# A 2496-point transform split 39 x 64 by index maps: one constant second-stage factor, and dispatch weights moved through it without transposes

## The chip, the cores and the metric

The kernel runs on one core of a Trainium2 chip. The metric is the device time of one execution in microseconds (us). Engines are named as in the profile: PE (TensorE matmuls; PEld are its weight loads), DVE (VectorE), ACT (ScalarE), POOL (GpSimd), and SP (SyncE), whose queue issues every DMA of this kernel. All arithmetic is float32 or its single-pass form fp32r.

## What is computed

A circular convolution along the sequence (by a real FFT, a filter and the inverse), and on its output a soft mixture of experts with 8 experts of 4 slots:

```
X = np.fft.rfft(x, axis=1)                 # x: 8 x 2496 x 256
y = np.fft.irfft(X * (filt_r + 1j * filt_i)[None], n=2496, axis=1)
x = y.reshape(19968, 256)
logits = x @ phi                           # 19968 x 32
d = exp(logits - logits.max(0));  d /= d.sum(0) + 1e-09
slot_input = d.T @ x                       # 32 x 256, "dispatch"
slot_out[e] = max(slot_input[e] @ w1[e], 0) @ w2[e]
c = exp(logits - logits.max(1));  c /= c.sum(1) + 1e-09
out = c @ slot_out                         # "combine"
```

## The kernel before

The tokens of a batch never leave the spectrum: the filtered spectrum is kept (tiles `y`), the logits of the spectrum are transformed back to tokens, and the dispatch weights of the tokens are transformed to the spectrum, where they are contracted with `y`.

**The transform.** Token n is written 64*s1 + s2. Stage one is a 39-point transform over s1, of which 20 values t = 0..19 are kept (the others are conjugates). Stage two is, for each t, a product with a 128x128 factor `b_t[:, t]` (64 values of s2, real and imaginary, against 64 bins, real and imaginary). The twiddle between the stages depends on t, so the 20 factors differ. At the start `build_b` (L641) makes 19 of them from two constant matrices and a cosine and a sine per row, one ACT multiply (L647, tile `bt`) and one DVE multiply-add (L648) each; the constants arrive in `be_t` and `b_t[:, 0]` by `load_b` (L688). Their transposes, which the inverse needs, are made later by `build_minv` (L650): four PE transposes, an ACT copy and a small POOL copy for each of 5 quarters.

**Startup.** Batch 0 goes through `first_unit` (L285): 11 units of 4 matmuls (L291) with a PSUM tile from `ps_s1` (2 buffers), each copied to `spec` by ACT (even units, L298) or DVE (odd, L296). A unit of `build_b` is written behind each of the first ten. Then `turn_ash` (L300) transposes `spec`, which needs all 11 units. Ahead of it, three matmuls (L705) on a tile of zeros run on PE while nothing has been loaded.

**The main loop** (L763) has 80 slots, 10 for each batch. A slot runs `x_unit` (L358): 4 matmuls (L365), two DVE multiplies with the filter tables `fr_t` and `fi_t` (L378, L379), a DVE or POOL add (L381), a POOL subtraction (L382), and for the first slot of a batch the Nyquist bin (L384); two slots later `t_unit` (L386) transposes the result into `y` (L392, L394) and makes logits of it (L403). Beside it go stage-one units of later batches: ACT and POOL split x into a high and a low part (`xh` L323, `xl` L324), three matmuls (L334), a copy (L335), a DMA to DRAM, and a DMA back in the order that stage two needs (`ash`, L355). The tables come by `load_tables` (L663), two values of t at a time.

**The chains.** For each group of batches, (0,1), (2,3), (4,5), (6), (7), `chain` (L416) is cut into pieces by `yield`, two of which are run after each slot. It turns logits to tokens (`v1` L449 with `minv_t`, `v` L469, `lg` L476), takes maxima, makes the weights `d` (L514, L515), turns them to the spectrum (`u` L532, `u2` L549, `dt` L563, `dd` L579), sums them (`z` L587), contracts them with `y` (`s` L607) and makes the row softmax (L628 to L636). `dt` has for each batch and t a matmul that loads 32 columns of `u2` as weights and streams `b_t[:, t]`; its result lies the wrong way round, so `dd` transposes it.

**The tail.** The expert weights (`w`, 64 DMAs of 256 KB, L746 and L748) are put into buffers that `y`, `ash` and the filter tables leave, so they wait for the last `x_unit` and the `s` of the last groups. Then the experts run (L833 to L863) and the combine writes the output, 20.4 MB.

What stands where on each engine is decided by a scheduler that simulates the program; each engine, SP too, then works its list in order.

Of the kernel before, what the change touches and what calls it, by code (L numbers as in the profile page):

```python
# [54 lines left out]
WM = 3  # L55
MV = 6
# [17 lines left out]
def freq_of(t, h, m):  # L74

    if t == 0:
        return N1 * m if h == 0 else None
    return N1 * m + (t if h == 0 else N1 - t)


def shape_constants():
# [10 lines left out]
    bm = np.zeros((N2, 2, NT, 2, 2, 32))  # L92
    for t in range(NT):
        for h in range(2):
            for m in range(32):
                f = freq_of(t, h, m)
                if f is None:
                    continue
                ph = 2 * np.pi * ((f * s2) % SEQ) / SEQ
                co, si = np.cos(ph), np.sin(ph)  # L100
                bm[:, 0, t, 0, h, m] = co
                bm[:, 0, t, 1, h, m] = -si
                if t:
                    sg = 1.0 if h == 0 else -1.0
                    bm[:, 1, t, 0, h, m] = sg * si
                    bm[:, 1, t, 1, h, m] = sg * co
    ph = np.pi * (s2 % 2)
    bm[:, 0, 0, 1, 0, 0] = np.cos(ph)
    bm = bm.reshape(P, NT, P)
    be = np.zeros((2, N2, 2, 2, 2, 32))  # L110
    for h in range(2):
        sg = 1.0 if h == 0 else -1.0
        for m in range(32):
            ph = 2 * np.pi * (((m + h) * s2) % N2) / N2
            co, si = np.cos(ph), np.sin(ph)
            be[0, :, 0, 0, h, m] = co
            be[0, :, 0, 1, h, m] = -si
            be[0, :, 1, 0, h, m] = sg * si
            be[0, :, 1, 1, h, m] = sg * co
            be[1, :, 0, 0, h, m] = -sg * si  # L120
            be[1, :, 0, 1, h, m] = -sg * co
            be[1, :, 1, 0, h, m] = co
            be[1, :, 1, 1, h, m] = -si
    tw = 2 * np.pi * np.repeat(s2, 2)[:, None] * np.arange(NT)[None] / SEQ
    bt = np.concatenate([bm[:, 0], be[0].reshape(P, P), be[1].reshape(P, P), np.cos(tw), np.sin(tw)], axis=1)
    for t in range(1, NT):
        full = be[0].reshape(P, P) * np.cos(tw[:, t : t + 1]) + be[1].reshape(P, P) * np.sin(tw[:, t : t + 1])
        assert np.abs(full - bm[:, t]).max() < 1e-12
    bh = bm[:, 0, :].copy()
    bh[:, 0] *= 0.5  # L130
    bh[:, 64] *= 0.5
# [16 lines left out]
    wt0 = np.full((P, 1), SCALE)  # L148
    wt0[0] = wt0[64] = SCALE / 2
    put("wt0", wt0)  # L150
    put("bh", bh)
# [27 lines left out]
    return cst.astype(f), off, w1q.astype(f), bt.astype(f)  # L179


CST, OFF, W1Q, BMAT = shape_constants()
KP = N2 + 2


def filter_layout(filt, special_zero):

    idx = np.array([[[freq_of(t, h, m) or 0 for m in range(32)] for h in range(2)] for t in range(NT)])
    a = filt[idx.reshape(NT, 64)]
    a = np.ascontiguousarray(a.reshape(NT, 64, 2, P).transpose(3, 0, 2, 1))  # L190
    if special_zero:
        a[:, 0, :, 0] = 0
    return a.reshape(P, NT * 2 * 64)
# [27 lines left out]
def fft_soft_moe(ctx, tc, x, fr, fi, fny, phi, w1, w2, cst, w1q, bmat, out):  # L221
# [136 lines left out]
    def x_unit(b, c):  # L358
# [4 lines left out]
        for k in range(2):  # L363
            for dh in range(2):
# [3 lines left out]
                    b_t[:, t0 + k, :],  # L368
# [14 lines left out]
        if c == 0:  # L383
            dve.tensor_tensor(out=yt[:, 0:2, 1, 0], in0=ps[:, 0:2, 1, 0], in1=fny_t, op=ALU.mult)  # L384
# [31 lines left out]
    def chain(g):  # L416
# [25 lines left out]
        for t0 in range(0, NT, 7):  # L442
            n = min(7, NT - t0)
            pv = psum([P, 7, KP // 2, 2], f"v1_{g}_{t0}")
            for t in range(t0, t0 + n):
                for b2 in range(nb):
                    for h in range(2):
# [4 lines left out]
                            minv_t[:, t, h * KP : (h + 1) * KP],  # L452
# [100 lines left out]
        NR = NT // 4  # L553
        dt = wk.tile([P, nb * NR, P], F32, tag="ca", name=f"dt_{g}", bufs=1)
        for r0 in range(0, nb * NR, 4):
            n = min(4, nb * NR - r0)
            pd = psum([P, 4, P], f"dt_{g}_{r0}")
            for r in range(r0, r0 + n):
                b2, tr = divmod(r, NR)
                for j in range(4):  # L560
                    t = 4 * tr + j
                    th, ti = divmod(t, HT)
                    pe.matmul(  # L563
                        pd[32 * j : 32 * j + 32, r - r0, :],
                        u2[:, ti, b2, th, :],
                        C("bh") if t == 0 else b_t[:, t, :],
                        start=True,
                        stop=True,
                    )
            act.copy(dt[:, r0 : r0 + n], pd[:, 0:n])  # L570
# [4 lines left out]
        for r0 in range(0, nb * NR, 4):
            n = min(4, nb * NR - r0)
            pd = psum([P, 4, P], f"dd_{g}_{r0}")
            for r in range(n):
                pe.transpose(pd[:, r, :], dt[:, r0 + r, :], ident)  # L579
            dve.tensor_copy(ddf[:, r0 * P : (r0 + n) * P], pd.rearrange("k r q -> k (r q)")[:, 0 : n * P])  # L580
# [4 lines left out]
        for b2 in range(nb):
            for j in range(4):
                pe.matmul(  # L587
                    pz[32 * j : 32 * j + 32, :], dd[:, b2, 0, :], C("e0"), start=(b2 == 0), stop=(b2 == nb - 1)
                )
# [14 lines left out]
        for b2, b in enumerate(bs):  # L604
            for t in range(NT):
# [35 lines left out]
    def build_b(c):  # L641

        for t in range(max(2 * c, 1), 2 * c + 2):
            sin_t = be_t[:, 2 * P + NT + t : 2 * P + NT + t + 1]
            cos_t = be_t[:, 2 * P + t : 2 * P + t + 1]
            tmp = x0p.tile([P, P], F32, tag="bt", name=f"bt_{t}", bufs=3)
            act.mul(tmp, be_t[:, P : 2 * P], sin_t)  # L647
            dve.scalar_tensor_tensor(out=b_t[:, t], in0=be_t[:, 0:P], scalar=cos_t, in1=tmp, op0=ALU.mult, op1=ALU.add)  # L648

    def build_minv(i):  # L650

        pm = ps_c.tile([P, 4, P], F32, tag="c", name=f"minv_{i}")
        for k in range(4):
            pe.transpose(pm[:, k], b_t[:, 4 * i + k, :], ident)
        ts = slice(4 * i, 4 * i + 4)
        act.mul(minv_t[:, ts, 0:P], pm, SCALE)
        if i == 0:
            act.mul(minv_t[:, 0, 0:P], pm[:, 0], C("wt0"))
        pad = minv_t[:, ts, P:].rearrange("c t (k r) -> c t k r", r=2)
        last_k = minv_t[:, ts, P - 2 : P].rearrange("c t (o r) -> c t o r", o=1).broadcast_to([P, 4, KP - N2, 2])  # L660
        pool_e.tensor_copy(pad, last_k)
# [26 lines left out]
    def load_b():  # L688
        sp.dma_start(b_t[:, 0], bmat[:, 0:P])
        sp.dma_start(be_t, bmat[:, P:])  # L690

    be_t = x0p.tile([P, 2 * P + 2 * NT], F32, name="be_t", bufs=1)
# [296 lines left out]
```

## Time and profile before

| what | before |
|---|---|
| median of 3 runs (lowest, highest) | 410.76 us (410.0, 410.95) |
| the profiled execution | 411.57 us |
| its span, first to last instruction | 409.8 us |
| PE, PEld busy | 372.0, 295.6 us |
| DVE, ACT, POOL busy | 279.0, 222.5, 201.1 us |
| moved by DMA | 103.81 MB |
| mean granted PE clock | 0.974 |

The profile has a page, which groups instructions by line, and views that answer a question: the timeline (start, duration, engine, line, operation), the chain of waits (the work that ended last, followed back; each piece with its start and duration), groups of instructions (count, busy time, mean duration, idle time ahead of them), and busy times in chosen stretches. A float32 matmul leaves two records on PE, a transpose or an fp32r matmul one.

### The profile page before, as it was taken

How to read it: one execution, taken by the hardware profiler on the slowest of the kernel's cores; microseconds unless marked ns; L12 is line 12 of the kernel's file. 1: busy time of each engine (PE TensorE's matmuls, PEld its weight loads, DVE VectorE, ACT ScalarE, POOL GpSimd, SP SyncE). 2: the span in 40 equal slices, each digit the busy share in tenths (PEclk: the TensorE clock that was granted, in tenths of full speed). 3: DMA queues.
4: the chain of work that ended last, by engine and by line, in shares of the span. 5: the costliest groups of instructions: out<-in, count | busy, mean ns of one | idle time of the engine just before them, and what ended most of it. 6: DMA issues, size and time to landing. Idle time of an engine off the chain costs nothing.

```text
span 409.8 us, 12706 instructions
## 1 busy us (share of the span) xinstructions
PE 372.0 (91%) x5155; PEld 295.6 (72%) x5155; DVE 279.0 (68%) x500; ACT 222.5 (54%) x479; POOL 201.1 (49%) x234
## 2 busy tenths in 40 slices
PE   6899999989998999999998999989998799988940
PEld 3788888868686867886877688779677534677830
DVE  4566788776999925778997567895549422587740
ACT  5777877766667475855781233461256210466630
POOL 0368979985775586865952155572120300443000
PEclk9999999999999999999999999998998999999985
DMA  7999899998689787987768033333089799199996
GB/s 250 357 279 309 266 332 310 309 369 275 178 258 314 234 254 223 299 300 226 239 194 297 5 106 108 106 98 106 2 298 375 242 281 323 78 416 412 415 416 275
DMA packets 57917, 103.81 MB, mean 253 GB/s; under 512 B 5551, under 2 KB 34607, under 8 KB 55683
## 3 DMA queue, kind: packets, MB, share of 16 engines
q1 hardware_dynamic: 57859, 103.00, 75.4%
q8 instruction: 41, 0.67, 0.7%
q14 instruction: 17, 0.14, 0.1%
HBM read 62.87 MB, written 40.12 MB: 251 GB/s over the span
## 4 chain that ended last, share of the span: by engine, by line
PE 65%; DVE 13%; DMA 10%; ACT 5%; issue 2%; SPq 0%; DVEq 0%; ACTq 0%
PE x L365 16%; PE s L334 11%; PE t L392 7%; DMA w<-in_w 6%; PE out L922 5%; PE s L607 4%; PE l L403 4%; DMA out<-ob 3%; PE dt L563 3%; PE v L449 2%; DVE t L379 2%; DVE yt L378 2%; PE u L532 2%; DVE d L514 2%; PE lg L476 2%
## 5 line engine op out<-in xcount | busy, mean ns | idle before, releaser
L324 POOL TENSOR_TENSOR xl<-xt,xh 117x512 fp32r<-117x512 f32 x77 | 103.6, 1353 | 36.6 <-ACT xh L323 34.0
L365 PE MATMUL x<-b_t,ash 128*128 128x128 f32 x640 | 91.3, 284 | 3.0 <-DVE t L379 2.0
L365 PEld LDWEIGHTS x<-b_t,ash 128*128 128x128 f32 x640 | 81.2, 194 | 12.0 <-issue 5.2
L382 POOL TENSOR_TENSOR yt<-yt,t 128x256 f32<-128x256 f32 x80 | 64.9, 812 | 47.7 <-DVE t L379 30.7
L378 DVE TENSOR_TENSOR yt<-x,fr_t 128x512 f32<-128x512 f32 x80 | 54.8, 685 | 30.4 <-PE x L365 21.1
L394 ACT COPY y<-t 128x512 f32<-128x512 f32 x80 | 46.4, 592 | 37.1 <-PE t L392 31.3
L323 ACT CAST xh<-xt 117x512 fp32r<-117x512 f32 x77 | 47.8, 622 | 29.5 <-PE s L334 19.8
L379 DVE TENSOR_TENSOR t<-x,fi_t 128x512 f32<-128x512 f32 x80 | 54.2, 678 | 0.0
L381 DVE TENSOR_TENSOR yt<-yt,t 128x256 f32<-128x256 f32 x60 | 49.7, 836 | 0.6
L392 PE MATMUL t<-cst_t,yt 128*128 128x128 f32 x320 | 48.5, 276 | 0.0
L335 ACT COPY at<-s 120x512 f32<-120x512 f32 x77 | 45.0, 588 | 1.1 <-PE s L334 1.0
L392 PEld LDWEIGHTS t<-cst_t,yt 128*128 128x128 f32 x320 | 37.1, 141 | 6.5 <-issue 2.7
L334 PE MATMUL s<-xh,w1h 117*120 117x512 f32 x77 | 35.3, 459 | 1.9 <-ACT at L335 1.8
L922 PE MATMUL out<-so_h,st 32*128 32x256 f32 x312 | 30.2, 299 | 3.8 <-ACT st L876 3.2
L381 POOL TENSOR_TENSOR yt<-yt,t 128x256 f32<-128x256 f32 x20 | 16.2, 811 | 32.3 <-DVE t L379 26.0
L334 PE MATMUL s<-xl,w1h 117*120 117x512 f32 x77 | 30.8, 400 | 0.1
L334 PE MATMUL s<-xh,w1l 117*120 117x512 f32 x77 | 30.5, 396 | 0.0
L931 DVE COPY ob<-out 128x512 f32<-128x512 f32 (+1 forms) x40 | 25.2, 672 | 6.3 <-PE out L922 4.9
L922 PEld LDWEIGHTS out<-so_h,st 32*128 32x128 f32 x312 | 23.9, 183 | 6.7 <-ACT st L876 3.5
L922 PE MATMUL out<-so_l,st 32*128 32x256 f32 x312 | 28.0, 277 | 0.0
L931 ACT COPY ob<-out 128x512 f32<-128x512 f32 (+1 forms) x40 | 21.3, 580 | 11.4 <-PE out L922 8.5
L403 PE MATMUL l<-yt,phi_t 128*32 128x128 f32 x640 | 27.1, 278 | 0.4 <-ACT y L394 0.2
(121 smaller groups left out, 576.6 us busy)
## 6 DMA issues: line engine op xcount, KB each, us to landing
xt<-in_x SPq DMA_DIRECT2D x35, 512.0 KB, 5.7
ash<-a_dram SPq DMA_DIRECT2D x70, 256.0 KB, 4.1
out<-ob SPq DMA_DIRECT2D x17, 1024.0 KB, 9.1
a_dram<-at SPq DMA_DIRECT2D x70, 240.0 KB, 5.0
w<-in_w SPq DMA_DIRECT2D x64, 256.0 KB, 5.5
xt<-in_x SPq DMA_DIRECT2D x18, 256.0 KB, 3.1
out<-ob SPq DMA_DIRECT2D x5, 512.0 KB, 12.8
c_dram<-lg SPq DMA_DIRECT2D x2, 643.5 KB
```

Of the source, the lines that this page charges most:

```text
L323: act.copy(xh, xs)
L324: pool_e.tensor_tensor(out=xl, in0=xs, in1=xh.bitcast(F32), op=ALU.subtract)
L334: pe.matmul(ps, w, xx, start=(n == 0), stop=(n == 2))
L365: pe.matmul(ps[:, 2 * k + dh].rearrange("q r c -> q (r c)"), ash[:, k, dh * P : (dh + 1) * P], b_t[:, t0 + k, :], start=True, stop=True,)
L378: dve.tensor_tensor(out=yt, in0=ps, in1=frv, op=ALU.mult)
L379: dve.tensor_tensor(out=t2, in0=ps[:, :, ::-1, :], in1=fiv, op=ALU.mult)
L381: add.tensor_tensor(out=yt[:, :, 1, :], in0=yt[:, :, 1, :], in1=t2[:, :, 1, :], op=ALU.add)
L382: pool_e.tensor_tensor(out=yt[:, :, 0, :], in0=yt[:, :, 0, :], in1=t2[:, :, 0, :], op=ALU.subtract)
L392: pe.transpose(pt[:, k, dh, :], yt[:, c % 2, 2 * k + dh].rearrange("q r c -> q (r c)"), ident)
L394: act.copy(y, pt.rearrange("k p h d -> k p (h d)"))
L922: nc.tensor.matmul(prs[k][:, mm, :], st[q, n // 2, c0 : c0 + P], (so_h, so_l)[n % 2][q, :], start=(n == 0), stop=(n == 3),)
L931: copy(ob[:, nm * k : nm * (k + 1), :], prs[k])
```

## The change

Tokens and bins are mapped so that the twiddle is 1: token (64*s1 + 39*s2) mod 2496, bin t + 39*m with m = (c - t/39) mod 64. The host arranges x and gathers the output by these maps. Then:

- one constant 128x128 factor `b` serves all t; `b_t`, `be_t`, their DMAs, `build_b` and `build_minv` go. The inverse reads the constants `minv` and (for t = 0) `minv0`. The first constant load has 256 columns in place of 129.
- the 64 bins of a t include bins above 1248; there the table holds the mirrored bin, and the imaginary part changes its sign: `load_tables` now has a POOL multiply by -1 on pieces of `fi_t`, 29 in all, 64 of 128 columns for each t of 1 to 19. The Nyquist multiply (L384) goes.
- the dispatch weights go through `b` as one wide matmul per up to 512 columns, with `b` as weights and `u2` streamed; the result is `dd` the right way round, so `dt` and the transposes go. ACT copies it; a DVE multiply halves two rows of t = 0.
- `first_unit` takes its PSUM tiles in turn from two pools (4 buffers in place of 2), and one warm-up matmul runs in place of three.

```
-WM = 3
-MV = 6
+WM = 1
+def token_of(s1, s2):
+    return (N2 * s1 + N1 * s2) % SEQ
+def bin_of(t, c):
+    m = (c - t * pow(N1, -1, N2)) % N2
+    return t + N1 * m
...
+    f = np.array([[bin_of(t, c) for c in range(N2)] for t in range(NT)])
+    a = filt[np.where(f > SEQ // 2, SEQ - f, f)]
+    a[0, N2 // 2 + 1 :] = 0
...
-        ps = ps_s1.tile([P, 2, 2, QP], F32, tag="s1", name=f"s0_{u}")
+        pool, tag = ((ps_s1, "s1"), (ps_x, "x"))[u % 2]
+        ps = pool.tile([P, 2, 2, QP], F32, tag=tag, name=f"s0_{u}")
...
-                    b_t[:, t0 + k, :],
+                    C("b"),
...
-        if c == 0:
-            dve.tensor_tensor(out=yt[:, 0:2, 1, 0], in0=ps[:, 0:2, 1, 0], in1=fny_t, op=ALU.mult)
...
-                            minv_t[:, t, h * KP : (h + 1) * KP],
+                            C("minv" if t else "minv0", h * KP, (h + 1) * KP),
...
-        dt = wk.tile([P, nb * NR, P], F32, tag="ca", name=f"dt_{g}", bufs=1)
...
-                    pe.matmul(
-                        pd[32 * j : 32 * j + 32, r - r0, :],
-                        u2[:, ti, b2, th, :],
-                        C("bh") if t == 0 else b_t[:, t, :],
...
-            act.copy(dt[:, r0 : r0 + n], pd[:, 0:n])
...
-                pe.transpose(pd[:, r, :], dt[:, r0 + r, :], ident)
-            dve.tensor_copy(ddf[:, r0 * P : (r0 + n) * P], pd.rearrange("k r q -> k (r q)")[:, 0 : n * P])
...
+        dd = wk.tile([P, HT, nb, 2, SLOTS], F32, tag="cb", name=f"dd_{g}", bufs=1)
+        for t0 in range(0, HT, SA):
...
+            pe.matmul(
+                pd[:, 0:n],
+                C("b"),
+                u2[:, t0 : t0 + n].rearrange("k t b h e -> k t (b h e)"),
...
+            act.copy(dd[:, t0 : t0 + n].rearrange("k t b h e -> k t (b h e)"), pd[:, 0:n])
+            if t0 == 0:
+                dve.tensor_scalar(
+                    out=dd[:, 0, :, 0, :], in0=dd[:, 0, :, 0, :], scalar1=C("wh"), scalar2=None, op0=ALU.mult
+                )
...
-    def build_b(c):
...
-    def build_minv(i):
...
+        for t in range(lo, hi):
+            for c0, c1 in flip_runs(t) if t else ():
+                sl = fi_t[:, t, :, c0:c1]
+                pool_e.tensor_scalar(out=sl, in0=sl, scalar1=-1.0, scalar2=None, op0=ALU.mult)
...
-        if c == 1:
-            load_b()
...
-            sp.dma_start(cst_t[:, 0 : P + 1], cst[:, 0 : P + 1])
+            sp.dma_start(cst_t[:, 0 : 2 * P], cst[:, 0 : 2 * P])
...
-        if u < CPB:
-            build_b(u)
...
-            if 0 <= n - MV < NT // 4:
-                build_minv(n - MV)
```

`flip_runs(t)` gives the one or two stretches of columns of t whose bin lies above 1248.

Three places show how the lists of the engines change. A row is: line, operation, tile written, tiles read, shape, and a count. Line numbers of the changed kernel are its own; numbers in the names count tiles.

**ACT, from the start**, before. `bt` is half of a factor, `spec` the copy of a unit of batch 0, `xh` the high part of x of batch 1:

```order
L647 ACTIVATE bt_251<-be_t 128x128
L298 COPY spec<-s_0_164 128x2x12x20
L647 ACTIVATE bt_254<-be_t 128x128
L647 ACTIVATE bt_263<-be_t 128x128
L647 ACTIVATE bt_266<-be_t 128x128
L647 ACTIVATE bt_275<-be_t 128x128
L298 COPY spec<-s_2_185 128x2x12x20
L647 ACTIVATE bt_278<-be_t 128x128
L298 COPY spec<-s_4_209 128x2x12x20
L323 CAST xh_0_322<-xt_0_152 117x512
```

and in the changed kernel:

```order
L280 ACT_TABLE_LOAD
L280 COPY spec<-s_0_167 128x2x12x20
L280 COPY spec<-s_2_179 128x2x12x20
L280 COPY spec<-s_4_191 128x2x12x20
L280 COPY spec<-s_6_203 128x2x12x20
L305 CAST xh_0_268<-xt_0_146 117x512
L305 CAST xh_1_272<-xt_0_146 117x512
L280 COPY spec<-s_8_215 128x2x12x20
L280 COPY spec<-s_10_227 128x2x8x20
```

Fourteen `bt` stood ahead of the first copy of `spec`; none is left, and the copies stand first.

**POOL, from the start**, before (`xl` is the low part of x of batch 1, `yt` the filtered spectrum of batch 0):

```order
L324 TENSOR_TENSOR xl_0_323<-xt_0_152,xh_0_322 117x512
L324 TENSOR_TENSOR xl_1_327<-xt_0_152,xh_1_326 117x512
L324 TENSOR_TENSOR xl_2_333<-xt_1_156,xh_2_332 117x512
L324 TENSOR_TENSOR xl_3_346<-xt_1_156,xh_3_345 117x512
L324 TENSOR_TENSOR xl_4_352<-xt_2_160,xh_4_351 117x512
```

and in the changed kernel, where `fi_t` is the imaginary filter table:

```order
L616 TENSOR_SCALAR fi_t<-fi_t 128x2x23
L616 TENSOR_SCALAR fi_t<-fi_t 128x2x9
L306 TENSOR_TENSOR xl_0_269<-xt_0_146,xh_0_268 117x512
L616 TENSOR_SCALAR fi_t<-fi_t 128x2x32
L616 TENSOR_SCALAR fi_t<-fi_t 128x2x5
L616 TENSOR_SCALAR fi_t<-fi_t 128x2x27
L306 TENSOR_TENSOR xl_1_273<-xt_0_146,xh_1_272 117x512
L616 TENSOR_SCALAR fi_t<-fi_t 128x2x28
L616 TENSOR_SCALAR fi_t<-fi_t 128x2x4
L616 TENSOR_SCALAR fi_t<-fi_t 128x2x32
L306 TENSOR_TENSOR xl_2_279<-xt_1_153,xh_2_278 117x512
L306 TENSOR_TENSOR xl_3_295<-xt_1_153,xh_3_294 117x512
```

The sign changes, each behind the load of its table, are mixed in among the first ten low parts.

**PE, dispatch of the third group** (batches 4 and 5), before. The tiles named `u_2` here are `u2` of the program, `cst_t` holds constants (identity, halved factor):

```order
L549 MATMUL u_2_8_4076<-cst_t,u_3906 128x128 x2
L563 MATMUL dt_0_4081<-cst_t,u_2_4032 32x128
L563 MATMUL dt_0_4081<-b_t,u_2_4032 32x128 x15
L563 MATMUL dt_4_4099<-b_t,u_2_4032 32x128 x4
L563 MATMUL dt_4_4099<-cst_t,u_2_4032 32x128
L563 MATMUL dt_4_4099<-b_t,u_2_4032 32x128 x11
L563 MATMUL dt_8_4117<-b_t,u_2_4032 32x128 x8
L579 MATMUL dd_0_4150<-cst_t,dt_4080 128x128 x4
L579 MATMUL dd_4_4156<-cst_t,dt_4080 128x128 x4
L579 MATMUL dd_8_4162<-cst_t,dt_4080 128x128 x2
L587 MATMUL z_4166<-cst_t,dd_4149 32x1 x8
```

and in the changed kernel:

```order
L529 MATMUL u_2_8_3890<-cst_t,u_3720 128x128 x2
L537 MATMUL dd_0_3895<-u_2_3846,cst_t 128x512
L537 MATMUL dd_4_3899<-u_2_3846,cst_t 128x512
L537 MATMUL dd_8_3902<-u_2_3846,cst_t 128x256
L555 MATMUL z_3927<-cst_t,dd_3894 32x1 x8
```

Forty small matmuls and ten transposes become three wide matmuls, at the same place between `u2` and `z`.

More of the change, by code (lines that the diff above doesn't have):

```diff
@@ L43 @@
 NM = BATCH * SQ // P
+KP = N2 + 2
 XC = 4
@@ L90, in shape_constants @@
             w1[:, 1, t] = -np.sin(th)
[L92 to L131, printed above, removed]
+    th = 2 * np.pi * (np.outer(s2, N1 * np.arange(N2)) % N2) / N2
+    co, si = np.cos(th), np.sin(th)
+    bm = np.zeros((N2, 2, 2, N2))
+    bm[:, 0, 0], bm[:, 0, 1], bm[:, 1, 0], bm[:, 1, 1] = co, -si, si, co
+    bm = np.where(np.abs(bm) < 1e-12, 0.0, bm).reshape(P, P)
+    wh = np.ones((P, 1))
+    wh[0] = wh[N2 // 2] = 0.5
+    minv = np.zeros((P, KP * 2))
+    minv[:, 0:P] = SCALE * bm.T
+    minv[:, P:] = np.tile(minv[:, P - 2 : P], (1, KP - N2))
     blocks = []
@@ L147, in shape_constants @@
     put("id", np.eye(P))
[L148 to L151, printed above, removed]
+    put("b", bm)
+    put("wh", wh)
+    put("minv", minv)
+    put("minv0", wh * minv)
     put("w1d", w1d.reshape(KR, 2 * PK * NT))
@@ L178, in shape_constants, with filter_layout, flip_runs @@
     f = np.float32
[L179 to L193, printed above, removed]
+    return cst.astype(f), off, w1q.astype(f)
+CST, OFF, W1Q = shape_constants()
+def filter_layout(filt):
+    f = np.array([[bin_of(t, c) for c in range(N2)] for t in range(NT)])
+    a = filt[np.where(f > SEQ // 2, SEQ - f, f)]
+    a[0, N2 // 2 + 1 :] = 0
+    return np.ascontiguousarray(a.reshape(NT, N2, 2, P).transpose(3, 0, 2, 1)).reshape(P, NT * 2 * N2)
+def flip_runs(t):
+    out = []
+    for c in range(N2):
+        if bin_of(t, c) > SEQ // 2:
+            if out and out[-1][1] == c:
+                out[-1] = (out[-1][0], c + 1)
+            else:
+                out.append((c, c + 1))
+    return out
 def x_layout(x):
-    s2 = np.array([[run_of(i, j) for i in range(NI)] for j in range(PK)])
-    a = x.reshape(BATCH, N1, N2, DIM)[:, :, s2]
+    s1 = np.arange(N1)
     full = np.zeros((BATCH, P, NI, DIM), x.dtype)
-    full[:, 0:KR] = a.transpose(0, 2, 1, 3, 4).reshape(BATCH, KR, NI, DIM)
+    for j in range(PK):
+        for i in range(NI):
+            full[:, j * N1 : j * N1 + N1, i] = x.reshape(BATCH, SEQ, DIM)[:, token_of(s1, run_of(i, j))]
     return full
@@ L587, in chain @@
                 pe.matmul(
[L588 removed]
+                    pz[32 * j : 32 * j + 32, :], dd[:, 0, b2, 0, :], C("e0"), start=(b2 == 0), stop=(b2 == nb - 1)
                 )
@@ L639, in chain @@
             sp.dma_start(c_dram[g], lg_t)
-    def build_b(c):
[L643 to L648, printed above, removed]
-    def build_minv(i):
[L652 to L661, printed above, removed]
     def load_tables(c):
@@ L686, in split_next @@
                 next_x()
[L688 to L692, printed above, removed]
     spec = x0p.tile([P, 2, NT, P], F32, name="spec", bufs=1)
@@ L769, in fft_soft_moe @@
             if n == CPB:
-                sp.dma_start(cst_t[:, P + 1 :], cst[:, P + 1 :])
+                sp.dma_start(cst_t[:, 2 * P :], cst[:, 2 * P :])
             if n == ASH:
```

47 lines of the change are left out of this document (11 added, 36 removed).

## The prediction

> **What bounds the kernel now.** I read the page first, then busy times by stretch, then the chain of waits inside each stretch, and rows of groups where a price was needed. The page gives PE the largest share:
>
> ```profile
> PE 372.0 (91%) x5155; PEld 295.6 (72%) x5155; DVE 279.0 (68%) x500; ACT 222.5 (54%) x479; POOL 201.1 (49%) x234
> ```
>
> A share is an average, so the stretches come next. The columns are stretch and length, then busy us and instructions of PE, PEld, DVE, ACT and POOL, the granted PE clock, DMA share and GB/s:
>
> ```profile
> 10.00:22.30 12.30, 10.26 (x76) 9.03 (x76) 6.95 (x13) 8.97 (x17) 3.73 (x3) 1.00 1.03 346
> 22.30:86.50 64.20, 64.20 (x555) 54.78 (x556) 48.24 (x70) 48.31 (x97) 55.61 (x55) 1.00 0.94 307
> 110.00:131.00 21.00, 20.05 (x285) 15.45 (x285) 20.31 (x29) 15.07 (x31) 14.75 (x13) 1.00 0.86 270
> 298.00:320.00 22.00, 20.24 (x390) 16.28 (x386) 16.55 (x50) 12.38 (x35) 2.10 (x3) 0.92 0.99 344
> 320.00:325.00 5.00, 4.34 (x99) 2.99 (x97) 1.63 (x5) 0.86 (x4) 1.55 (x3) 1.00 0.52 165
> 325.00:349.40 24.40, 22.04 (x275) 10.06 (x269) 5.56 (x13) 3.15 (x6) 1.73 (x8) 1.00 0.98 289
> 356.00:400.00 44.00, 35.06 (x621) 30.98 (x621) 30.58 (x58) 25.30 (x58) 10.61 (x28) 0.95 1.00 407
> ```
>
> From 22.3 to 86.5 PE never pauses: there a matmul less is its time less. From 110 to 131 DVE sets the pace. From 298 on the DMA is full (weights to 349.4, the output after 356), but for a hole at 320 to 325. Before 22.3 PE has gaps, and the chain of waits names what ends them:
>
> ```profile
> 2.58 3.67 DMA be_t<-in_bmat
> 6.28 4.19 ACT bt L647 x14
> 10.47 0.86 ACT spec L298
> 11.38 1.17 PE s L291 x8
> 12.56 0.99 ACT spec L298
> ...
> 20.30 1.17 PE s L291 x8
> 21.49 0.73 ACT spec L298
> 22.26 1.09 PE ash L305 x8
> ```
>
> The first copy of `spec` waits on ACT behind fourteen `bt`, which wait for `be_t`. With two PSUM buffers PE then waits for every second copy, and the transposes start at 22.26.
>
> **The change part by part.** Signs are changes of the time.
>
> *Start: -4.2.* Neither `be_t` nor `bt` is ahead of the copies any more, and four PSUM buffers let PE run on. What is late next is x itself, then PE:
>
> ```profile
> xt<-in_x SPq DMA_DIRECT2D x18, 256.0 KB, 3.1
> 1.58 5.31 PE L705 MATMUL warm_up<-warm 128*128 128x512 f32 x6 [1.58 <-DVE warm L702]
> 6.72 1.94 PE L291 MATMUL s<-w1q_t,xt 117*128 117x120 f32 x16
> 13.60 2.06 PE L291 MATMUL s<-w1q_t,xt 117*128 117x120 f32 x16 [0.18 <-ACT spec L298]
> 106.06 0.86 PE lg L476 x2
> ```
>
> The first x tile is issued at about 1.2 and lands 3.1 later, at 4.3. A later one of 256 KB takes 0.73 at 359 GB/s or so (346 in the row of 10 to 22.3), so DMA stays ahead of PE, which needs 1.03 for a unit (16 records, two units, 2.06). The warm-up tells that PE is slow at first: six records of 512 columns take 5.31, 0.88 each, where `lg` does such a record in 0.43. By 6.72 it is at full speed. With one warm-up matmul the same clock time should free it, since units of x follow almost at once: 1.2 units at half speed from 4.3 to 6.7, then 9.8 units of 1.03 to 16.8, the last copy 0.73, transposes at 17.6: -4.7. If it stays slow for 3.4 longer, 2.8 units are done by 10.1, the rest takes 8.4, and the transposes start at 19.3: -3.0. I take -4.2, nearer to the first.
>
> The Trainium skill, "TensorE: Matmul & The Clock Gate", Part 1 (The HAM clock gate), says that the array starts at half clock and is released by about 3.4 us of sustained work, counted in a free-running window; the rows of the warm-up agree with the factor of two. By that rule a shorter warm-up, which cost nothing, is a loss, and a window that holds the pause between warm-up and x may not count: this is the rival "cold start" below.
>
> *Transposed factors: -2.2.*
>
> ```profile
> L654 PE MATMUL minv<-cst_t,b_t 128*128 128x128 f32 x20 | 3.2, 272 | 0.0
> 42.49 0.44 PE minv L654 x4
> ```
>
> Twenty transposes at 0.11 (0.44 for four) stand in the stretch without a PE gap. ACT and POOL lose their parts too.
>
> *Dispatch in the first group: -1.8; in the second and third: -2.7 each.* Before, in the third group:
>
> ```profile
> 283.43 2.08 PE dt L563 x64
> 285.53 0.59 ACT dt L570
> 286.17 0.67 PE dd L579 x4
> 286.87 1.66 DVE dd L580 x3
> 288.57 4.52 PE s L607 x80
> ```
>
> PE, ACT, PE, DVE follow one another with nothing else ahead in PE's list: 5.14 from `dt` to `s`. Three matmuls over 512, 512 and 256 columns replace this; by the row of `lg` (0.86 for 512) they take 2.15. Copies on ACT and the halving on DVE run beside the later ones, and `z` costs 0.3: 2.45 in place of 5.14, -2.7. The second group shows the same serial chain. In the first group other work fills the waits, and only PE's own time counts: 80 records at 0.57 for 16 and ten transposes at 0.11 make 3.95, less 2.15.
>
> ```profile
> 140.71 0.57 PE dt L563 x16
> 223.17 1.49 PE dt L563 x48
> 224.69 0.60 ACT dt L570
> 225.33 0.67 PE dd L579 x4
> 226.02 1.66 DVE dd L580 x3
> ```
>
> Most of the DVE copies that go stand outside the stretch that DVE paces; with the Nyquist multiplies I count that relief at nothing (bound -1.2).
>
> *Last groups: -2.2.* All of these shifts pass to the weights, whose DMAs wait for the last slot. The hole at 320 to 325 is SP's wait for `s`:
>
> ```profile
> SPq L748 <- PE s L607: 5.0, 2, 4.7
> 314.11 2.36 PE dt L563 x40
> 320.61 2.19 PE s L607 x40
> ```
>
> In the fourth group 6.5 pass from `dt` to `s`. Without the turn this is 1.07 (640 columns), doubled at most while the clock is low, a copy, a halving, and the fifth group's `u` in between: some 3 earlier. That closes the hole, which is worth 0.48 x 5 = 2.4 of DMA time; I take 2.2 (bounds 0 and 2.4). The fifth group ends earlier by as much and stays ahead of the queue.
>
> *Sign changes on POOL: +1.5.* No row shows a multiply by a constant on POOL. The nearest:
>
> ```profile
> L895 POOL TENSOR_TENSOR cr<-c,cst_t 117x96 f32<-117x96 f32 x8 | 2.8, 352 | 0.0
> L890 POOL COPY cr<-c 117x96 f32<-117x96 f32 x8 | 2.1, 266 | 0.8 <-PE ct L903 0.7
> L661 POOL COPY minv_t<-minv_t 128x16 f32<-128x16 f32 x5 | 0.8, 194 | 0.0
> 16.54 3.73 POOL L324 TENSOR_TENSOR xl<-xt,xh 117x512 fp32r<-117x512 f32 x3 [16.10 <-ACT xh L323]
> ```
>
> A piece has 42 columns on average, so 0.19 to 0.35; I take 0.23, 6.7 for 29, less the five small copies: +5.9 of POOL. POOL has 8.6 idle from 22.3 to 86.5 and 8.6 from 10 to 22.3, and its work may now begin near 13, not 16.54. Queued behind a sign change are `xl`, for these PE's third matmul of a unit, and in order behind it everything on PE. Walking both lists with these durations PE waits once or twice for `xl`, 0.6 to 1.7 in all. Bounds are 0 and +5.9 (none of the idle time usable).
>
> *At nothing:* the larger constant loads replace 212 KB of factors; ACT's copies of `dd` replace those of `dt`; the same matmuls with another right side cost the same.
>
> Sum: -4.2 - 2.2 - 1.8 - 2.7 - 2.7 - 2.2 + 1.5 = **-14.3**. The profiled execution took 411.57 (span 409.8 and 1.8 around it), so 397.3; it lies 0.8 above the median of the runs, 410.76, so the forecast for a median is **396.5**.
>
> **The rivals.**
> - *Cold start.* PE stays at half speed through a further window or two, since the single warm-up matmul ends before x lands. For it: the slow records last until 6 even with PE busy from 1.58. Against it: units follow in under a microsecond. One window costs 1.2 more than my term; at half speed for all eleven units the transposes start at 4.3 + 22.7 + 0.7 = 27.7, a term of +5.4 in place of -4.2: 406. One window, the likelier: 397.7.
> - *POOL takes the place of PE* from 13 to 86. For it: POOL's 55.61 of 64.2 with the PE list shortened by 6.4 there. Against it: part of the sign changes fit ahead of 22.3. Price +5.9 in place of +1.5: 401.
> - *The start is fed by DMA*: its share is 1.03 from 10 to 22.3, so x of batch 1 and the tables come no earlier, and PE, though started, waits. Three of the 4.2 are lost: 399.5. Against it: SP's waits name compute, and 0.2 MB go.
> - *Slower.* One mechanism: sign changes much dearer than the copies, at POOL's start, with `xl` and so PE queued behind them. It decides where 29 of them exceed POOL's idle time and the whole gain, 17 + 15.8 = 33, or 1.1 each; then 412 or more. The 512-column row of `xl` (1.24 each) reaches that, at twelve times the columns.
> - *It doesn't do what it says*: PE's list shows `dt` and the transposes gone, and the wide matmuls stand directly ahead of `z`, so this is left at nothing.
>
> **How the numbers follow.** Forecast as summed 0.59; cold start 0.12; POOL 0.14; DMA 0.08; slower 0.05; some mixture that ends within 0.2% 0.02. The likeliest gives 396.5. The lower end takes every bound at its best: -4.7, -2.2, -1.8, -2.7 twice, -2.4, -1.2, 0 = -17.7, or 393.1; I write 392.8. The upper end takes in POOL's 401 and a cold window with it: 402.5. A measurement of this kernel can tell some 0.2% from no change: faster 0.93, same 0.02, slower 0.05.
>
> **What would show it.** Right: the transposes of `spec` at 17 to 19.5; no `minv` on PE; `dd` to `s` in about 2.5 in groups two and three; sign changes at 0.19 to 0.35 and no PE gap over 2 in total before 80; the weights' DMA starting some 12 earlier and running without a hole. Wrong: `xl` named as PE's releaser again and again up to 80; records of L291 at twice 0.13 beyond 10; or a DVE stretch that is longer than the 21 of before.

## The result, and the profile after

| | before | after |
|---|---|---|
| median of 4 runs (lowest, highest) | 410.86 us (410.0, 412.75) | 398.1 us (397.09, 399.22) |
| the profiled execution, and its span | 411.57, 409.8 us | 398.73, 397.0 us |
| PE, DVE, ACT, POOL busy | 372.0, 279.0, 222.5, 201.1 us | 367.3, 267.8, 215.3, 206.7 us |

The changed kernel takes 0.9684 of the time (95% interval 0.9639 to 0.9729). Run once more as it is (r1 below) it gave 0.9643 (0.959 to 0.9696). Where a run below is set against it, its ratio is taken as the mean of these two, 0.9664; one per cent of the kernel before is 4.1 us. The two differ by 1.7 us, so a difference of about 2 us between ratios is not resolved. Executions over 1.5% above the fastest of a kernel are left out of the ratios, and the profiles of e2 and e8 below are the longest executions of their sets (398.72 and 401.55), so where their marks stand is read as spread only.

The timeline of PE in the changed kernel shows the start (columns: start, duration, engine, line, operation, out<-in, count, and the idle time ahead with what ended it):

```profile
1.56 2.07 PE L648 MATMUL warm_up<-warm 128*128 128x512 f32 x2 [1.56 <-DVE warm L645]
4.09 12.26 PE L273 MATMUL s<-w1q_t,xt 117*128 117x120 f32 x88 [0.46 <-DMA xt<-in_x]
...
17.67 1.04 PE L287 MATMUL ash<-cst_t,spec 128*128 128x128 f32 x8
```

The eleven units run without a pause in 12.26, but not at one pace. The busy times by stretch (stretch, length, then PE, PEld, DVE, ACT, POOL with their instructions, granted clock, DMA share, GB/s) show twice as many records of PE in the second 4.60 us as in the first:

```profile
4.09:8.69 4.60, 4.60 (x22) 4.60 (x22) 0.82 (x1) 0.98 (x1) 0.00 (x0) 1.00 0.93 303
8.69:13.29 4.60, 4.60 (x43) 4.60 (x42) 2.13 (x3) 2.46 (x3) 0.00 (x0) 1.00 1.07 383
```

By the starts of the records, the first 21 follow one another every 0.22 us on average and the rest every 0.112, so a unit of 8 records takes 0.89 at full pace and the slow ones cost 21 x 0.107 = 2.2. The granted clock of this view reads 1.00 in both rows and doesn't show it. PE ends the units at 16.36; the last copies of `spec` stand on ACT behind two `xh` and end at 17.38, and the transposes come at 17.67 in place of 22.26. The same view shows the stretch behind the start and, from 343 on, the output:

```profile
22.30:80.00 57.70, 54.65 (x465) 45.15 (x465) 45.50 (x63) 40.06 (x82) 55.70 (x68) 1.00 0.93 315
343.00:388.00 45.00, 41.14 (x579) 37.42 (x573) 29.09 (x54) 24.37 (x54) 9.68 (x24) 0.73 0.95 390
```

Before, PE had no pause at all in the first of these stretches, and POOL was busy 49.70. Now 3.05 of 57.7 are pauses of PE, and POOL, busy 55.70, has 2.0 left. In the output phase the granted clock is 0.73 and the DMA share 0.95 (0.95 and 1.00 before, from 356 to 400). The third group's dispatch, and the sign changes in the groups of instructions on POOL (busy, mean ns | idle):

```profile
272.17 2.45 PE L537 MATMUL dd<-u,cst_t 128*128 128x512 f32 x6
274.73 0.31 PE L555 MATMUL z<-cst_t,dd 128*32 128x1 f32 x16
275.08 4.52 PE L575 MATMUL s<-y,dd 128*32 128x256 f32 x80
```

```profile
L616 POOL TENSOR_SCALAR fi_t<-fi_t 128x64 f32<-128x64 f32 x9 | 3.5, 393 | 0.0
L616 POOL TENSOR_SCALAR fi_t<-fi_t 128x4 f32<-128x4 f32 x2 | 0.5, 228 | 0.0
```

From `dd` to `s` it is 2.91 in place of 5.14. `s` of the third group starts at 275.08 in place of 288.57 (-13.5; some of it is no gain of the change, since the profile of before has a granted clock of 0.66 from 275 to 280). The first output matmul is the mark that I use for the end of everything ahead of the output; the last weights' matmuls (`o`) stand in front of it:

```profile
317.93 3.64 PE L770 MATMUL h<-w,sit 128*32 128x512 f32 x32 [0.32 <-DVE sit L760]
...
334.07 1.91 PE L787 MATMUL o<-w,ht 128*32 128x256 f32 x26
...
337.76 0.50 PE L859 MATMUL out<-so_h,st 32*128 32x256 f32 x5 [0.46 <-ACT so_h L799]
```

Before, the first such row stood at 352.93: -15.2. At the end of the span 12.8 are left, so 2.4 went while the output was written.

### The profile page after: what moved, and what is told of

The parts are those of the page before. It is cut to its first block, busy times and chain, and to the rows that moved or that the text cites. A ratio compares the mean times of both kernels' runs of the same rounds, so it can differ in the third digit from the quotient of the medians.

```text
span 397.0 us, 11950 instructions
## 1 busy us (share of the span) xinstructions
PE 367.3 (93%) x4797; PEld 292.8 (74%) x4797; DVE 267.8 (67%) x465; ACT 215.3 (54%) x454; POOL 206.7 (52%) x258
## 5 line engine op out<-in xcount | busy, mean ns | idle before, releaser
L306 POOL TENSOR_TENSOR xl<-xt,xh 117x512 fp32r<-117x512 f32 x77 | 102.0, 1332 | 17.8 <-ACT xh L305 17.3
L347 PE MATMUL x<-cst_t,ash 128*128 128x128 f32 x640 | 89.9, 281 | 3.2 <-issue 1.7
L347 PEld LDWEIGHTS x<-cst_t,ash 128*128 128x128 f32 x640 | 80.2, 191 | 12.8 <-issue 6.6
L364 POOL TENSOR_TENSOR yt<-yt,t 128x256 f32<-128x256 f32 x80 | 64.8, 812 | 39.4 <-DVE t L361 21.2
L305 ACT CAST xh<-xt 117x512 fp32r<-117x512 f32 x77 | 47.6, 623 | 30.5 <-PE s L316 13.5
L363 DVE TENSOR_TENSOR yt<-yt,t 128x256 f32<-128x256 f32 x60 | 51.0, 860 | 0.5
L859 PE MATMUL out<-so_h,st 32*128 32x256 f32 x312 | 36.2, 355 | 3.1 <-ACT st L813 2.7
L859 PE MATMUL out<-so_l,st 32*128 32x256 f32 x312 | 34.3, 331 | 0.0
L825 POOL TENSOR_TENSOR c<-cl,r_all 117x352 f32<-117x352 f32 x8 | 6.2, 798 | 53.5 <-PE ct L839 46.8
L859 PEld LDWEIGHTS out<-so_h,st 32*128 32x128 f32 x312 | 29.8, 234 | 5.5 <-ACT st L813 3.1
L868 ACT COPY ob<-out 128x512 f32<-128x512 f32 (+1 forms) x40 | 21.5, 579 | 16.9 <-PE out L859 14.6
L316 PE MATMUL s<-xh,w1l 117*120 117x512 f32 x77 | 30.6, 397 | 0.0
```

The costliest lines, as they stand in the source:

```text
L305: act.copy(xh, xs)
L306: pool_e.tensor_tensor(out=xl, in0=xs, in1=xh.bitcast(F32), op=ALU.subtract)
L316: pe.matmul(ps, w, xx, start=(n == 0), stop=(n == 2))
L347: pe.matmul(ps[:, 2 * k + dh].rearrange("q r c -> q (r c)"), ash[:, k, dh * P : (dh + 1) * P], C("b"), start=True, stop=True,)
L363: add.tensor_tensor(out=yt[:, :, 1, :], in0=yt[:, :, 1, :], in1=t2[:, :, 1, :], op=ALU.add)
L364: pool_e.tensor_tensor(out=yt[:, :, 0, :], in0=yt[:, :, 0, :], in1=t2[:, :, 0, :], op=ALU.subtract)
```

## The experiments

All are the changed kernel with one edit. Ratios are to the kernel before, run on the same chip in turn. A single profile doesn't place a mark closely: the first `v1` of the changed kernel stood at 89.53 and 89.27 in two profiles, of another kernel run twice (sign changes on ACT, below) at 87.14 and 88.84, and at 92.23 in one of e8, whose list on PE is that of the changed kernel up to about 114 us. So shifts of 3 us or less in one profile are not taken for a finding; ratios decide. The changed kernel itself ran in the first set and beside e6, e7 and e8 only.

**The changed kernel once more (r1_as_changed).** No edit.

> The changed kernel once more, unaltered, beside the others of this set. The first profile lost 2.4 us while the output is written, with a granted clock of 0.5 from 355 to 380 us and the DMA share down to 0.72. If that is a matter of one execution: the next profile has a shorter half-clock stretch, a DMA share near 1.0 throughout, and a median of 396 to 398. If the changed kernel brings it about: the same stretch again, and a median of 398 or more.

Measured: 396.93 (394.88 to 401.12), ratio 0.9643 (0.959 to 0.9696). The busy times by stretch, first of the first profile of the changed kernel, then of this one:

```profile
355.00:360.00 5.00, 5.00 (x53) 4.70 (x53) 3.25 (x7) 2.89 (x7) 2.40 (x6) 0.50 1.01 416
...
370.00:375.00 5.00, 5.00 (x51) 4.70 (x51) 2.92 (x6) 2.60 (x6) 0.00 (x0) 0.50 0.83 342
375.00:380.00 5.00, 5.00 (x99) 4.72 (x96) 2.91 (x6) 2.43 (x5) 0.00 (x0) 0.76 0.72 288
```

```profile
355.00:360.00 5.00, 4.89 (x83) 4.34 (x81) 4.50 (x9) 3.84 (x9) 2.40 (x6) 1.00 1.02 419
...
370.00:375.00 5.00, 4.25 (x71) 3.71 (x70) 3.81 (x6) 3.13 (x7) 0.00 (x0) 1.00 1.01 411
375.00:380.00 5.00, 4.62 (x80) 4.07 (x80) 3.27 (x7) 2.69 (x6) 0.00 (x0) 1.00 1.02 419
```

In the first profile PE is at half clock for some 20 us; it is busy nearly all the time with 53 records in 5 us where 83 go through at full clock, and after 365 it no longer keeps the output's DMA full. In the second the clock is full and so is the DMA. This profile's span is 395.2, 14.6 less than before. The loss of 2.4 belongs to an execution, not to the change; the clock's dips differ from profile to profile in the other kernels too.

**The old dispatch (e1_old_dispatch).**

```
-        dd = wk.tile([P, HT, nb, 2, SLOTS], ...)
-            pe.matmul(pd[:, 0:n], C("b"), u2[:, t0 : t0 + n]...)
-            act.copy(dd[:, t0 : t0 + n]..., pd[:, 0:n])
+                    pe.matmul(pd[32 * j : 32 * j + 32, r - r0, :], u2[:, ti, b2, th, :], C("bh" if t == 0 else "b"), ...)
+            act.copy(dt[:, r0 : r0 + n], pd[:, 0:n])
+                pe.transpose(pd[:, r, :], dt[:, r0 + r, :], ident)
+            dve.tensor_copy(ddf[:, r0 * P : (r0 + n) * P], ...)
```

> The changed kernel, but with the dispatch weights going through the factor as before (32-column matmuls, ACT copy, transposes, DVE copy). Theory (the terms of the prediction, 1.8 + 2.7 + 2.7 for the first three groups and 2.2 for the hole in the weights' DMA): +9.4 on the changed kernel's 398.1, so about 407.5, with dd to s back at about 5.1 us in the second and third group. Rival one (the shift of 13.5 us that the trace shows by s of the third group comes in part from the freed copies and the freed start, not from the dispatch): +5 or less, 403. Rival two (the output phase lost 2.4 us because the kernel now runs with fewer pauses and the clock is taken down at its end): the middle of the trace moves by 9 but the end by 7 only, 405, with the granted clock after 350 us back at 0.95.

Measured: 406.27 (405.18 to 408.22), ratio 0.9907 (0.9874 to 0.9939): +0.0243 to the changed kernel's 0.9664, 10.0 us, or 8.2 by the medians of the two first sets (406.27 less 398.1). The timeline of PE:

```profile
276.46 2.64 PE L544 MATMUL dt<-cst_t,u 128*32 128x128 f32 x80
279.27 1.09 PE L560 MATMUL dd<-cst_t,dt 128*128 128x128 f32 x8 [0.17 <-ACT dt L551]
280.71 0.44 PE L560 MATMUL dd<-cst_t,dt 128*128 128x128 f32 x2 [0.35 <-DVE dd L561]
281.31 0.30 PE L568 MATMUL z<-cst_t,dd 128*32 128x1 f32 x16 [0.16 <-DVE dd L561]
281.67 4.52 PE L588 MATMUL s<-y,dd 128*32 128x256 f32 x80
...
346.63 0.50 PE L872 MATMUL out<-so_h,st 32*128 32x256 f32 x5 [0.46 <-ACT so_h L812]
```

5.21 from `dt` to `s`, and the first output is 8.9 later than in the first profile of the changed kernel and 8.2 later than in r1 (338.47). The theory holds (9.4 forecast); 5 or less is out. At `s` of the first, second and third group the shifts are 5.1, 4.3 and 6.6 (2.8, 2.1 and 4.4 against r1), and 2.3 more (3.8) come in the last two groups. By these marks the dispatch of the first group gave the most and the second group nothing; the third gave 2.3 against either profile. Rival two is answered by r1.

**No sign changes (e2_no_flips).**

```
-        for t in range(lo, hi):
-            for c0, c1 in flip_runs(t) if t else ():
-                sl = fi_t[:, t, :, c0:c1]
-                pool_e.tensor_scalar(out=sl, in0=sl, scalar1=-1.0, scalar2=None, op0=ALU.mult)
```

> The changed kernel without the sign changes of the imaginary table (leaves out the mirrored bins' signs, so the values differ; the amount of the other work is the same). Theory (sign changes cost 1.5): 396.6. Rival one (they cost 0.34 us each, 9.9 in all, dearer than forecast, and POOL has no pause from 13 to 45 us; xl and PE queue behind them): the gain in front of 80 us is 3 or more, 395 or below, and v1 of the first group comes 3 us earlier than at 89.53. Rival two (the waits of the first 80 us are for x and its transfers, not for POOL): nothing, 398, and the same 3 us of PE gaps between 22.3 and 80.

Measured: 395.05 (392.8 to 398.72), ratio 0.9619 (0.9583 to 0.9656): 1.8 less than the changed kernel, with intervals that overlap. The stretch from 15 to 45, of the changed kernel, then of this one:

```profile
15.00:45.00 30.00, 27.91 (x219) 23.39 (x218) 20.99 (x30) 20.38 (x40) 29.49 (x47) 1.00 0.88 277
```

```profile
15.00:45.00 30.00, 29.84 (x252) 26.24 (x251) 21.17 (x31) 23.65 (x46) 25.52 (x23) 1.00 0.95 313
```

With the sign changes POOL is busy 29.49 of 30 and PE stands still for 2.1; without them POOL has 4.5 to spare and PE almost no pause (with the sign changes on ACT, below, it is the same). So they do cost PE about 2 there. About half of it is lost again behind 45: over the whole stretch from 22.3 to 80 PE pauses 2.0 without them (1.6 and 1.9 with them on ACT) and 3.05 and 2.42 with them on POOL. The pause is shown; whether it is worth 1.8 at the end is not resolved. `xl` is hardly what ends PE's waits: PEld waits 0.2 for it from 20 to 80 in the changed kernel. POOL's subtraction (`yt`, L364) stands late behind the sign changes, and DVE's multiply `t` waits for it (2.2, and 3.0 in r1); this wait is not in the lists of e2 and e11.

**Sign changes three times (e6_flips_three).** `+                for _ in range(3):` ahead of the multiply.

> Each sign change done three times (the value is the same as after one): 58 more POOL instructions of about 0.34 us, +20 us of POOL. If POOL paces the first 80 us (the rival of the prediction): +10 to +20, 408 to 418, with xl as what PE waits for. If the sign changes lie in POOL's idle time up to the amount that is there (from 13 to 80 us POOL has some 2 to 4 us idle, later tables reach into it): single ones cost 0 to 1.5 and this costs +5 to +10.

Measured: 416.97 (414.42 to 421.53), ratio 1.0127 (1.0075 to 1.0179), 20.0 over the changed kernel in the same set (396.93). Stretches, and what was waited for from 20 to 80 (engine, line and tile that waited, what ended it: us in total, times, longest):

```profile
15.00:45.00 30.00, 26.85 (x168) 21.59 (x167) 16.46 (x22) 17.58 (x34) 29.63 (x63) 0.83 0.76 238
45.00:80.00 35.00, 27.58 (x187) 20.44 (x186) 22.54 (x24) 16.60 (x33) 31.81 (x54) 0.85 0.72 222
```

```profile
DVE t L361 <- POOL fi_t L617: 10.6, 4, 3.3
ACT xh L305 <- POOL xl L306: 9.6, 8, 3.3
PE x L347 <- DVE t L361: 4.6, 2, 3.2
```

The 58 more are 19 us of POOL by their records, and the kernel is 20 us longer: from 15 to 70 POOL is busy 54.6 of 55, where the changed kernel leaves 2.5, so behind the first 29 there is almost no idle time left on POOL. The multiply `t` waits for the sign changes themselves, PE for `t`, and `xh` for `xl`. The granted clock is 0.83 and 0.85 there, where the changed kernel has 1.00; what brought it down, and how much of the 20 us it made, is not shown. This is the rival "POOL paces", one step beyond the change.

**The factors' transposes put back (e7_minv_again).**

```
+    def minv_again(i):
+        pm = ps_c.tile([P, 4, P], F32, tag="c", name=f"minv_{i}")
+        for k in range(4):
+            pe.transpose(pm[:, k], C("b"), ident)
+        act.mul(mvx, pm, SCALE)
...
+            if 0 <= n - 6 < NT // 4:
+                minv_again(n - 6)
```

> Twenty transposes of the factor and five ACT copies of 512 columns put back at the slots where the transposed factors were made before (their result is not used). Theory (PE has no pause there, so their own time counts): +2.2, about 400. Rival (PE is not what paces the first 80 us, so the 2.2 were never there): 0 to +0.5, 398.

Measured: 395.07 (394.74 to 396.97), ratio 0.9618 (0.9576 to 0.966). Twenty more transposes cost nothing: the time is 1.9 below that of the changed kernel in the same set, which is not resolved, but +2.2 is out. The timeline of PE and the stretch show where they went:

```profile
30.56 0.60 PE L623 MATMUL minv<-cst_t 128*128 128x128 f32 x4
...
34.86 1.04 PE L623 MATMUL minv<-cst_t 128*128 128x128 f32 x8
```

```profile
15.00:45.00 30.00, 29.84 (x242) 26.00 (x241) 20.83 (x30) 22.32 (x44) 29.73 (x47) 1.00 0.85 277
```

PE is busy 29.84 in place of 27.91 while POOL stays as full as it was: the transposes fill the pauses that POOL leaves on PE. Those lie mostly from 35 to 40 in the changed kernel (3.68 busy of 5). The first `v1` stands at 88.77, no later than 89.53 and 89.27. The 2.2 of the prediction are not there. In this run the transposes stand at 30.6 to 35.9; before the change they stood at 42.3 to 54.8, and what they would cost at that place is not shown.

**Transposes back, no sign changes (e10_minv_no_flips).** Both edits.

> The twenty transposes and five copies put back (which cost nothing beside the sign changes), now without the sign changes (leaves out the signs of the mirrored bins). If the transposes were hidden because POOL paced the stretch: here PE paces it, and v1 of the first group comes 2 us later than the 87.85 of the run without sign changes, the time 396 to 397 in place of 395. If they are hidden by PE's own small gaps: 87.9 again and 395.

Measured: 397.33 (395.1 to 399.08), ratio 0.9647 (0.9598 to 0.9697), 1.2 more than without the transposes, intervals overlapping. `v1` is at 90.33, 1.5 and 3.2 later than in the two profiles with the sign changes on ACT, which would be PE's time; but PE has pauses from 15 to 45 here too (28.77 busy), and the transposes stand later, at 36.3 to 49. The direction is that of the theory; neither it nor the size is resolved.

**Sign changes on DVE (e3_flips_dve) and on ACT (e11_flips_act, r2_flips_act).** `pool_e.tensor_scalar(out=sl, ...)` becomes `dve.tensor_scalar(out=sl, ...)`, or `act.mul(sl, sl, -1.0)`.

> The sign changes moved from POOL to DVE. If POOL's pace costs time in the first 80 us, this comes as low as the run without sign changes plus what DVE takes for 29 small pieces (45 of 57.7 us busy there; estimated at 0.1 us each, 3 in all, in its idle time): 395 to 397. If POOL's pace is hidden: 398, or slower by up to 1 where the copies of spec and the multiplies of x_unit queue behind them on DVE.

> The sign changes on ACT in place of POOL. If they cost 1.5 to 3 because POOL has no idle time from 13 to 80 us, ACT (20 of 30 us busy from 15 to 45) hides them: 395, as without them. If they then delay xh, which opens each unit of stage one, or the copies of spec: no gain, 397 to 399, with spec's transposes at 18.5 or later.

> The sign changes on ACT once more, unaltered, to tell a gain over the changed kernel from the spread of executions. If ACT hides them and POOL did not: a ratio to the kernel before of 0.958 to 0.963 again, below the 0.9684 and 0.9643 of the changed kernel's two sets. If the first set was luck: 0.964 to 0.969.

On DVE: 398.09 (394.3 to 400.04), ratio 0.9694 (0.9648 to 0.974): no gain. On ACT: 395.92 and 396.65, ratios 0.9606 (0.9557 to 0.9655) and 0.9623 (0.9578 to 0.9667): on average 0.9615, 2.0 less than the changed kernel, with overlapping intervals. PE is busy 29.89 and 29.92 from 15 to 45 with ACT, as without sign changes. Whether it is faster than the changed kernel these runs don't settle: e7, which only adds work to the changed kernel, stands at 0.9618 too. The timeline of DVE in e3:

```profile
15.19 2.54 DVE L616 TENSOR_SCALAR fi_t<-fi_t 128x64 f32<-128x64 f32 x3 [0.37 <-DMA fi_t<-in_fi]
...
18.48 1.85 DVE L616 TENSOR_SCALAR fi_t<-fi_t 128x56 f32<-128x56 f32 x3
...
26.30 0.35 DVE L616 TENSOR_SCALAR fi_t<-fi_t 128x40 f32<-128x40 f32 x3
```

and of POOL in e3:

```profile
15.15 5.14 POOL L306 TENSOR_TENSOR xl<-xt,xh 117x512 fp32r<-117x512 f32 x4 [14.71 <-ACT xh L305]
```

The estimate of 0.1 each held for the last row (0.12), where POOL was idle (from 25.8 to 27.9). While POOL ran `xl`, three took 2.54 and 1.85; the last copy of `spec` on DVE stands behind the first three, and the transposes are at 18.74, 1.1 later. The Trainium skill, "SBUF — State Buffer", section "SBUF: two separate sides", says that DVE and GpSimd share one pair of ports under an exclusive lock, so that one of them blocks for the other's whole instruction, where the DVE operation uses that pair. The rows agree: two `xl` of 1.28 each are 2.57, and the three sign changes that began with them took 2.54.

**Three warm-up matmuls (e4_warm3), and these with two PSUM buffers (e9_psum2_warm3).** `WM = 3`; in e9 also `ps_s1.tile(...)` for every unit.

> Three warm-up matmuls in place of one, all else as changed. If PE is slow at the start only because of the missing warm-up (it lost about 1.0 us to slow records from 4.09 on): units of x start at about 6.7 and the transposes of spec come at 6.7 + 11.3 + 0.7 = 18.7, 1.0 later than at 17.67, so 398 to 399. If the start is fed by x and its transfers further on, the time after 80 us is the same: 398.1. If a cold clock after one warm-up costs more than the wait for three, the transposes come earlier than 17.67 and the time is 397.

> First units with two PSUM buffers and three warm-up matmuls, as before; the factors stay constant, so no copies of theirs stand in front. Theory (start worth 4.2, of which the freed ACT list, which stays, is a part): the transposes of spec at 19 to 20.5 in place of 17.7, and v1 of the first group 1.5 to 3 later than at 89.3 to 89.5, the time 399. Rival (what paces the first 80 us is POOL and the transfers of x, which start no later with this): transposes later by as much, but v1 at 89.5 and the time as the changed kernel's, 397 to 398.

e4: 397.45 (396.12 to 400.83), ratio 0.9697 (0.966 to 0.9734), 1.4 more than 0.9664, intervals overlapping; transposes at 18.78, 1.1 later. Here the units start at 6.84 and run at full pace from 7.4, so three warm-ups save some 2 of the slow records' 2.2 and cost 2.75 by their later start. e9: 403.48 (401.29 to 406.68), ratio 0.9796 (0.9745 to 0.9848), 5.4 more. The timeline of PE in e9:

```profile
6.84 2.25 PE L272 MATMUL s<-w1q_t,xt 117*128 117x120 f32 x16
9.27 2.05 PE L272 MATMUL s<-w1q_t,xt 117*128 117x120 f32 x16 [0.18 <-ACT spec L279]
...
17.23 2.04 PE L272 MATMUL s<-w1q_t,xt 117*128 117x120 f32 x16 [1.46 <-ACT spec L279]
...
21.44 1.09 PE L286 MATMUL ash<-cst_t,spec 128*128 128x128 f32 x8
```

and of ACT:

```profile
15.17 1.14 ACT L304 CAST xh<-xt 117x512 fp32r<-117x512 f32 x2 [1.50 <-DMA xt<-in_x]
```

PE waits for copies of `spec` again, although no copies of factors are on ACT, and the transposes are at 21.44, 3.8 later. The longest wait (the 1.46) is for a copy that stands behind these two `xh`. `v1` is at 92.71, 3.2 to 3.4 later, and the first output at 342.43, 4.0 to 4.7 later. By the ratio, whose interval lies clear of the changed kernel's two, the start is real and goes through to the end; the rival that x feeds it is out.

**More early weights (e8_wl9).** `WL = 9` in place of 5.

> Nine buffers in place of five for weights that load before the last x_units (the change freed 20 KB of a partition that the 20 factors and their transposes had; 4 more tiles of 256 KB fit). The DMA share is 0.40 from 240 to 290 us and 1.0 from 290 to 330, so 1 MB less in the full stretch: by 0.64 us a tile at 412 GB/s, -2.5 us, 395.5. If the end of the weights is set by the last s and the buffers that it frees: no change, 398.

Measured: 397.46 (395.89 to 401.55), ratio 0.9686 (0.9632 to 0.974): no change. From `h` to the first output it takes 19.8 with five early tiles and with nine:

```profile
323.22 3.64 PE L770 MATMUL h<-w,sit 128*32 128x512 f32 x32 [0.32 <-DVE sit L760]
...
343.05 0.50 PE L859 MATMUL out<-so_h,st 32*128 32x256 f32 x5 [0.46 <-ACT so_h L799]
```

Before the change it was 21.2, with the last `o` drawn out to 3.29 over its weights, for which PEld waits 1.4. In r1 it is 21.1, the last `o` is drawn out to 3.19, and PEld waits 1.3 for them. So after the change the weights and the chain of the last groups and the experts end within about 1.3 us of one another, and buffers that bring the weights earlier can win no more than that; before it was nearly the same.

## Why the prediction was right

The forecast was 396.5 (392.8 to 402.5), the result 398.1. The sum of -14.3 stands against -12.8 by the spans of the first pair of profiles, with 2.4 lost to a half clock, and -14.6 by the span of r1. Part of this nearness is luck. By ratios the gain is 13.8, and the parts undone one by one give 5.4 for the start, nothing for the transposes, 10.0 for the dispatch and the last groups, less 1.8 for the sign changes, or 13.6: what the transposes did not bring, the start and the dispatch brought in excess. The intervals of the ratios are some 0.45% to each side, so these runs tell less than the 0.2% that the prediction counted on. By its own steps:

- **Start, -4.2: right in its sum, by luck in its parts.** The transposes came 4.6 earlier, at 17.67, where the nearer case said 17.6. But PE was slow up to 8.69 and not 6.7; a unit at full pace takes 0.89 and not 1.03 (a row of 16 records that lasts 2.06 also holds a slow first record behind a wait and the end of its last one); and the last copy ended 1.0 behind PE, with two `xh` ahead of it. These three cancel. Undoing buffers and warm-up together brings 3.8 of the 4.6 back (e9), but in e9 two `xh` take a place on ACT ahead of a copy, so the share of the freed ACT list is not shown. At the end buffers and warm-up are worth 5.4 (4.0 to 4.7 at the first output).
- **Transposed factors, -2.2: wrong.** The step said that PE never pauses there, so a matmul less is its time less. That was read from the kernel before. In the changed kernel POOL has almost no pause from 15 to 45 and PE has some 2 us of them (2.4 to 3.05 from 22.3 to 80), and the twenty transposes fit into these (e7). Two terms on one stretch, taken from one engine each, were summed as if that stretch kept its bound.
- **Dispatch, -1.8, -2.7, -2.7, and the last groups, -2.2: right.** Together 9.4; undone, 8.2 by medians, 10.0 by ratios, 8.2 to 8.9 at the first output. How they divide was less well placed: by e1 against the two profiles of the changed kernel the first group gave 5.1 and 2.8, where 1.8 was forecast, the second -0.8 and -0.7 and the third 2.3 twice, where 2.7 each were forecast, and the last two groups 2.3 and 3.8, where 2.2 was forecast. In the third the three wide matmuls take 2.45, not 2.15, and `dd` to `s` 2.91, not 2.45.
- **The hole in the weights' DMA: right.** It closed (the DMA share is 1.05 from 306 to 311 us, where the fifth group runs). The weights and the chain on PE end within 1.3 of one another, so the transfer alone does not set the time (e8).
- **Sign changes, +1.5: about right in size, but the price of one was low and the path another.** They took 228 to 456 ns by their records, 0.34 on average and 9.9 in all, not 0.23 and 6.7. POOL became full (29.49 of 30) and PE paused for 2; removal gave 1.8 by ratios, unresolved. The step queued `xl` and PE's third matmul behind them; the trace names POOL's subtraction `yt` and DVE instead. The sign "no PE gap over 2 in total before 80" did not come (3.05 and 2.42). The rival "POOL paces" (401) did not decide the time, but its mechanism is in the trace, and e6 shows that it starts right behind this change.
- **Cold start: it came, and other misses hid it.** PE lost 2.2 to slow records, up to 8.69, where the term had 1.2. In the eleven profiles with one warm-up the full pace begins at 7.4 to 10.0, or 3.3 to 5.7 behind the first unit; with three it begins at 7.4 and 7.5 (e4, e9), and before the change by 6.72. Three warm-ups still brought no gain, since the units start later with them (e4). The Trainium skill, "TensorE: Matmul & The Clock Gate", Part 1 (The HAM clock gate), gives some 3.4 us of sustained work until the release, in a window that runs freely; 3.3 to 5.7 of units agree with that if the single warm-up, 0.46 ahead of them, did not count, which no run here shows by itself.
- **DVE relief at nothing** and the larger constants were not tried by themselves.

## What to carry to other kernels

Price each term with the bound that the changed kernel will have: when one edit loads the second-busiest engine of a stretch, the gains of another edit on the busiest one can vanish into the pauses. A serial chain PE, ACT, PE, DVE that is replaced is worth what it shrinks by where nothing else is queued on PE (5.14 to 2.91 in the third group gave 2.3 at `s`); what it is worth where other work fills it these profiles don't settle (1.8 forecast in the first group, 5.1 and 2.8 seen). A unit's price is read from the starts of its records, not from the length of a row. When a transfer stops being late, look at once for what ends last now, before giving it more buffers.

## What the runs showed of the hardware

- POOL multiplies by a constant with 4 columns in 228 ns and with 64 in 393; ACT does the same in 211 and 265 (e11). On a straight line through the two, an estimate, some 0.21 of each is a cost per instruction: most of ACT's time and about half of POOL's longer one.
- With one warm-up matmul PE's first records of 120 columns came every 0.22 us on average up to 8.69 and every 0.112 after that; the profile's granted clock reads 1.00 throughout.
- A small multiply on DVE took 0.12 us each (40 columns) in a row where POOL was idle and 0.85 (64 columns) in one where POOL ran `xl` beside it (e3).
- The granted clock from 355 to 375, while the output is written, was 1.00 in one profile and 0.50 in another of the same program; the half clock cost time where PE, at 51 records in 5 us (370 to 375), no longer kept the output's DMA full.
